# A new order of instructions from the hand-over to the experts on, with two weight subtractions moved from VectorE to GpSimd

## The chip, the core and the metric

The kernel runs on one core of a Trainium2 chip. The metric is the device time of one execution in microseconds. The engines are named as the profile names them: PE is TensorE's matmul side and PEld its weight load, DVE is VectorE, ACT is ScalarE, POOL is GpSimd, SP is SyncE, which issues most DMAs.

## What is computed

Three stages follow each other on 3072 tokens (4 batches of 768) of width 320: a gated linear attention with 8 heads, a dense layer with a softmax gate and a layer norm, and a mixture of 8 experts in which each token goes to one expert alone. The last stage is the one around the change:

```python
logits = xn @ en.T / tau                 # xn, en: rows and expert vectors divided by their norms
expert_idx = np.argmax(logits, axis=1)
gate_w = probs[np.arange(N), expert_idx] # probs: softmax of the logits
for e in range(E):
    mask = expert_idx == e
    h = np.maximum(x[mask] @ w1[e], 0.0)              # 320 -> 1024
    out[mask] = gate_w[mask, None] * (h @ w2[e])      # 1024 -> 320
```

## The kernel before

**Two halves.** In the first half 24 groups of 128 tokens pass through attention, dense layer and routing. Their output rows (320 numbers, the gate, the expert's number) go to a table `ys` in HBM. Every matmul operand is held as a high part in fp32r (rounded by ACT) and a low part (the rest, by a subtraction), and a product is three matmuls. In the second half the eight experts are worked through in the order of their token counts (ranks 0 to 7); the program fixes the number of rows of each rank (496, 432, 448, 424, 360, 352, 328, 264). For each tile of up to 128 rows of a rank, GpSimd gathers the rows from `ys` with an indirect DMA (L1118, tile `xgr`), PE transposes them (L1129, `txr`), ACT and DVE split them (`exr`), PE multiplies with the first weights (m1, L1152 to L1161, tile `hpu`, eight column blocks f = 0 to 7 of some 8 matmuls), ACT takes the positive part as high part (L1184, tile `uu`), DVE makes the low part (L1190), PE multiplies with the second weights (m2, L1208 to L1210, tile `ypu`), ACT scales with the gate (L1215), and GpSimd scatters the rows to the output (L1222).

**From counts to a gather.** For each of 7 blocks of groups (four of 4 groups, one more of 4, then two of 2: blocks 0 to 6) the routing runs through a chain: the best expert of each row (L776 and the rows behind), its place among the expert's rows by a matmul with counts (L810 to L813, tile `pp`), that place read off (L817, L818), a key (L828 to L832, tiles `key` and `vr`), one-hot rows (L837, L839, tiles `ohr` and `ohv`; by GpSimd for blocks 0 to 5, by DVE for block 6), a matmul that inverts them (L845, `ip`), and an addition to the table `inv` (L848). From `inv` DVE takes the row numbers of the gathers (L1037 to L1041). The first three tiles of rank 0 need blocks 0 to 4 only, so they start early; this part of rank 0 is the unit u0. Its fourth tile of 112 rows (unit u1) and all later ranks need block 6, and so the last link of the chain.

**PE during the chain.** While block 6 goes through the chain, PE works on u0. There m1 writes to two PSUM banks in turn, so that block f+2 starts only when ACT and DVE have split block f. PE has 8 blocks of m1 and the first two of three tiles of m2 to do before it takes the transposition of the fourth tile of rank 0.

**Weights.** The five weight tiles of a rank (0 to 2 first weights, 3 and 4 second weights) come over SP (L1098) into a ring of four slots `raw`. ACT makes the high part (L1102), and an engine given in a table subtracts it (L1109; L1106 for tile 2, which has the work on 64 partitions), which frees the slot:

```python
    def w_lo(R, i, eng):
        if i == 2:
            eng.tensor_tensor(out=R.h[2][64:], in0=R.raw[2][64:], in1=R.h[2][64:].bitcast(F32), op=ALU.subtract)
        else:
            R.l[i] = pools[R.pool].tile([P, wsize(i)], F32R, tag=f"l{i}", name=f"l{R.name}_{i}")
            eng.tensor_tensor(out=R.l[i], in0=R.raw[i], in1=R.h[i].bitcast(F32), op=ALU.subtract)
```

**The order.** The kernel is recorded as steps (`plan.add`), each with an engine. A table `AT` gives each step a number, and the steps are written out in the order of these numbers, so that each engine's queue is that order and nothing is reordered at run time. The dependences stay; a step that isn't ready holds all that stands behind it on its engine. Queues touched by the change: PE, DVE, ACT, POOL and SP.

Of the kernel before, what the change touches and what calls it, by code (L numbers as in the profile page):

```python
# [24 lines left out]
E = 8  # L25
# [44 lines left out]
    "ld_c2": "386",  # L70
    "ld_e": "60",
    "set_m": "0",
    "set_z": "28",
    "sets": "1",
    "mk": "63",
    "mku": "520",
# [5 lines left out]
    "bad": "805",  # L82
    "badp": "904",
    "badc": "972",
    "neg": "64",
    "f_in": "546 70 429 10",
    "dec_in": "669 195 597 90",
    "whi": "708 248 668 680 130",
    "wlo": "725 572 704 738 380",
    "wd": "337",  # L90
    "emb1": "171",
    "emb2": "185",
    "embr": "244",
    "emb3": "261",
    "emb4": "279",
    "emb5": "293",
    "f_out": "141 266",
    "dec_out": "318 459",
    "wtr": "494 463 409 450 601 608 618 544",
    "wtc": "510 475 441 464 647 625 637 598",  # L100
    "ep": "576 662",
    "epc": "721",
    "ept": "731",
    "cmb": "1115",
    "eg": "751",
    "eohi": "760",
    "eolo": "827",
    "onefr": "31",
    "ohi": "451 405 413 421 569 545 561 553",
    "olo": "808 786 756 831 765 795 841 817",  # L110
    "cm": "910 915 921 927 933 1092 1099 1104",
    "fill": "62 79 96 114 154 251 289 298 419 477",
    "load_q": "30 115 87 359 332 531 908 1069 1322 1544 1726 1949 2120 2354 2531 2804 3009 3332 3600 3780 4050 4223 4450 4673",
    "load_n": "206 236 399 50 499 577 963 1159 1389 1578 1813 2024 2208 2420 2570 2876 3150 3397 3676 3816 4120 4310 4515 4738",
    "vprep": "355 371 534 385 616 699 1046 1244 1473 1661 1898 2124 2313 2504 2653 2995 3241 3481 3778 3900 4206 4394 4598 4843",
    "tprep": "351 370 533 162 615 698 1070 1275 1472 1667 1897 2121 2293 2503 2654 2960 3258 3485 3781 3925 4205 4393 4614 4822",
    "smat": "131 259 387",
    "pv": "374 436",
    "smm": "486 527",
    "pmul": "168 181 291 305 432 445 882 958 1043 1057 1296 1384 1527 1598 1711 1725 1923 1937 2094 2108 2328 2341 2505 2519 2785 2798 2994 3021 3306 3320 3574 3588 3754 3872 4024 4126 4204 4230 4435 4510 4758 4780 4878 4919 5062 5163 5343 5449",  # L120
    "state": "498 583 909 1100 1323 1738 1950 2144 2355 2535 3036 3333 3601 3804 4051 4462 4686 4891 5077 5356",
    "den": "400 540 902 1123 1316 1541 1776 1978 2161 2382 2532 2840 3113 3361 3629 3774 4044 4218 4449 4702 4933 5106 5384 5552",
    "og": "411 552 938 1135 1363 1553 1788 2000 2184 2394 2544 2852 3125 3373 3651 3790 4081 4285 4490 4714 4945 5128 5396 5564",
    "xdup": "437 578 962 1160 1388 1577 1818 2048 2212 2419 2569 2942 3156 3419 3702 3817 4122 4309 4514 4767 4989 5176 5460 5588",
    "xtr": "470 696 1065 1318 1413 1586 1839 2116 2252 2430 2584 3005 3185 3454 3776 3908 4219 4342 4530 4781 5008 5198 5476 5597",
    "xh": "485 727 1079 1334 1429 1597 1849 2130 2273 2449 2605 3026 3201 3494 3791 3935 4236 4353 4577 4791 5018 5209 5497 5619",
    "xl": "586 775 1098 1352 1447 1611 1863 2173 2287 2462 2627 3040 3219 3508 3812 3948 4249 4366 4591 4806 5051 5267 5511 5654",
    "mm1": "742 806 942 974 1113 1227 1372 1420 1601 1642 1770 1854 1984 2025 2220 2259 2397 2436 2684 2716 2893 2925 3108 3237 3421 3469 3644 3686 3867 3919 4103 4135 4311 4367 4545 4579 4748 4787 4943 4975 5130 5251 5444 5483 5658 5690 5860 5892",
    "negmax": "857 1019 1271 1502 1687 1899 2070 2303 2481 2760 2969 3282 3550 3730 4000 4179 4411 4622 4840 5026 5305 5527 5759 5937",
    "expo": "886 1047 1300 1539 1715 1927 2098 2332 2512 2789 3004 3310 3578 3758 4028 4213 4439 4651 4869 5055 5333 5556 5788 5966",  # L130
    "umul": "914 1074 1328 1573 1742 1954 2125 2358 2589 2815 3051 3337 3605 3823 4056 4260 4466 4677 4895 5081 5360 5584 5814 5992",
    "lnstat": "943 1102 1356 1602 1771 1982 2153 2393 2618 2844 3080 3365 3633 3851 4106 4289 4494 4706 4923 5110 5388 5613 5843 6022",
    "lnvar": "971 1136 1393 1631 1823 2011 2186 2424 2664 2873 3161 3394 3665 3888 4136 4318 4523 4735 4953 5151 5417 5650 5879 6067",
    "lnrs": "1000 1164 1422 1676 1852 2040 2216 2453 2693 2902 3288 3423 3694 3917 4164 4347 4552 4764 4982 5180 5446 5768 5908 6116",
# [8 lines left out]
    "inter": "514",  # L143
    "att": "845 1006 1260 1488 1675 1886 2057 2291 2468 2748 2957 3269 3538 3717 3987 4167 4398 4610 4828 5014 5292 5515",
    "mmp": "5722 5926",
    "rlog": "2020 2927 3685 4602 5478 6027 6222",
    "rnorm": "2068 2939 3722 4621 5490 6046 6234",
    "ridx": "2029 2935 3693 4647 5486 6035 6231",
    "rexp": "2140 2999 3800 4681 5550 6108 6304",
# [1420 lines left out]
```

## Time and profile before

| what | us |
|---|---|
| three runs: median (lowest to highest) | 524.79 (520.2 to 525.45) |
| the profiled execution, its own time | 522.23 |
| its span from the first to the last instruction | 520.4 |
| PE busy, of the span | 494.0 |
| DVE, ACT, POOL busy | 340.0, 275.0, 203.9 |

PE is the engine that is nearly always busy. The time is PE's work and the stretches in which PE waits, so the waits of PE, what ends them, and the granted clock are what is to be read.

### The profile page before, as it was taken

The page shows a single profiled execution, that of the slowest core. Times are in us where ns is not written, and L with a number is a line of the kernel's source. Part 1 is how long each engine was busy: PE and PEld are TensorE (multiplying, and loading weights), DVE is VectorE, ACT ScalarE, POOL GpSimd, SP SyncE. Part 2 cuts the span into 40 slices and gives each one's busy share as a digit, 9 for nine tenths or more (in the row PEclk, how much of TensorE's full clock was granted, in tenths as well). Part 3 has the DMA queues.
Part 4 walks back from the last instruction along what each step waited for, and adds up shares of the span by engine and source line. Part 5 has one row for each costly group of instructions (what it writes and reads, how often), then busy time and mean ns, then how long its engine had stood idle before and what let it go on. Part 6 is the DMA issues. An engine that isn't in the chain of part 4 may idle for free. (4 is left out here: it accounts for less than half of the span.)

```text
span 520.4 us, 14487 instructions
## 1 busy us (share of the span) xinstructions
PE 494.0 (95%) x5925; PEld 452.2 (87%) x5925; DVE 340.0 (65%) x735; ACT 275.0 (53%) x604; POOL 203.9 (39%) x350
## 2 busy tenths in 40 slices
PE   6869999999999999999999899999999999999991
PEld 5747998888899999889898789898999999999991
DVE  5997667777677587677778778677463655485120
ACT  3572555665656556666467565554543644565220
POOL 3221223266246247345315683656172444112021
PEclk9989999999999999999999899999999999999996
DMA  8962233343341253414041412835631861563000
GB/s 300 412 223 81 80 83 120 113 147 111 90 144 46 77 156 121 144 40 143 3 171 44 152 47 96 276 84 193 231 92 44 285 223 64 217 189 121 14 21 31
DMA packets 20139, 68.01 MB, mean 131 GB/s; under 512 B 2658, under 2 KB 6050, under 8 KB 19680
## 3 DMA queue, kind: packets, MB, share of 16 engines
q1 hardware_dynamic: 17120, 58.27, 33.5%
q0 software_dynamic: 2944, 8.73, 5.3%
q8 instruction: 49, 0.80, 0.7%
q14 instruction: 26, 0.21, 0.1%
HBM read 58.31 MB, written 8.72 MB: 129 GB/s over the span
## 5 line engine op out<-in xcount | busy, mean ns | idle before, releaser
L1222 POOL DMA_INDIRECT out_x<-you,sidx x28 | 30.8, 1099 | 95.5 <-ACT you L1215 82.9
L748 PE MATMUL Y<-OH,uh 128*128 128x328 f32 x192 | 63.4, 330 | 0.0
L1190 DVE SCALAR_TENSOR_TENSOR lu<-hpu,uu 128x384 fp32r<-128x384 f32 (+4 forms) x56 | 28.6, 519 | 53.0 <-ACT uu L1184 43.5
L750 PE MATMUL Y<-OH,ul 128*128 128x328 f32 x192 | 60.3, 314 | 0.2 <-DVE ul L740 0.2
L749 PE MATMUL Y<-OL,uh 128*128 128x328 f32 x192 | 60.4, 315 | 0.0
L1208 PE MATMUL ypu<-hr,uu 128*128 128x320 f32 (+4 forms) x192 | 60.1, 313 | 0.0
L1209 PE MATMUL ypu<-lr,uu 128*128 128x320 f32 (+4 forms) x192 | 59.3, 309 | 0.0
L1184 ACT ACTIVATE uu<-hpu 128x384 fp32r<-128x384 f32 (+7 forms) x64 | 30.4, 483 | 52.2 <-PE hpu L1161 40.0
L1109 DVE TENSOR_TENSOR lr<-raw,hr 128x1024 fp32r<-128x1024 f32 (+1 forms) x32 | 43.4, 1355 | 15.1 <-ACT hr L1102 15.1
L1210 PE MATMUL ypu<-hr,lu 128*128 128x320 f32 (+4 forms) x168 | 51.8, 309 | 0.0
L1102 ACT CAST hr<-raw 128x1024 fp32r<-128x1024 f32 (+1 forms) x40 | 45.2, 1134 | 10.5 <-DMA raw<-in_w 9.4
L736 ACT CAST uh<-tpu 128x512 fp32r<-128x512 f32 x48 | 27.7, 586 | 38.7 <-PE tpu L732 38.4
L704 ACT ACTIVATE e<-H,nmx 128x1024 f32<-128x1024 f32 x24 | 26.8, 1117 | 40.2 <-DVE nmx L699 40.2
L1118 POOL DMA_INDIRECT xgr<-ys,gidx x28 | 36.5, 1302 | 27.3 <-issue 8.9
L699 DVE TENSOR_REDUCE nmx<-H 128x1 f32<-128x1024 f32 x24 | 29.4, 1224 | 26.1 <-PE H L695 24.5
L1157 PE MATMUL hpu<-exr,hr 128*128 128x384 f32 (+7 forms) x128 | 43.7, 341 | 0.0
L1158 PE MATMUL hpu<-exr,lr 128*128 128x384 f32 (+7 forms) x128 | 42.5, 332 | 0.0
L1159 PE MATMUL hpu<-exr,hr 128*128 128x384 f32 (+7 forms) x128 | 42.4, 332 | 0.0
L686 PE MATMUL H<-WH,xh 128*128 128x512 f32 x96 | 40.7, 424 | 1.2 <-DVE u L709 1.1
L740 DVE TENSOR_TENSOR ul<-tpu,uh 128x512 fp32r<-128x512 f32 x48 | 32.4, 687 | 12.6 <-ACT uh L736 12.5
L687 PE MATMUL H<-WL,xh 128*128 128x512 f32 x96 | 37.9, 395 | 0.1
L748 PEld LDWEIGHTS Y<-OH,uh 128*128 128x128 f32 x192 | 36.2, 189 | 2.0 <-ACT yr L766 0.2
(230 smaller groups left out, 1351.3 us busy)
## 6 DMA issues: line engine op xcount, KB each, us to landing
qk<-in_qkT SPq DMA_DIRECT2D x24, 512.0 KB, 4.2
raw<-in_w SPq DMA_DIRECT2D x24, 512.0 KB, 4.7
nat<-in_nat SPq DMA_DIRECT2D x24, 484.0 KB, 3.7
raw<-in_w SPq DMA_DIRECT2D x16, 640.0 KB, 5.3
ys<-yr SPq DMA_DIRECT2D x5, 772.0 KB, 5.0
raw<-in_w_out SPq DMA_DIRECT2D x2, 1280.0 KB, 9.3
raw<-in_w_in SPq DMA_DIRECT2D x3, 512.0 KB, 6.4
raw<-in_w_in SPq DMA_DIRECT2D x1, 1024.0 KB, 8.3
```

The lines of the kernel that those rows point to most:

```text
L686: T.matmul(out=o, lhsT=xh[:, kk, :], rhs=WH[:, kk, f], start=(kk == 0), stop=False)
L748: T.matmul(out=yp, lhsT=uh, rhs=OH[:, k, :], start=(k == 0), stop=False)
L749: T.matmul(out=yp, lhsT=uh, rhs=OL[:, k, :], start=False, stop=False)
L750: T.matmul(out=yp, lhsT=ul, rhs=OH[:, k, :], start=False, stop=(k == 7))
L1102: A.copy(out=R.h[i], in_=R.raw[i])
L1109: eng.tensor_tensor(out=R.l[i], in0=R.raw[i], in1=R.h[i].bitcast(F32), op=ALU.subtract)
L1157: T.matmul(out=o, lhsT=R.h[k][:, fs_], rhs=xh[:, k, tk], start=(k == 0), stop=False)
L1158: T.matmul(out=o, lhsT=R.l[k][:, fs_], rhs=xh[:, k, tk], start=False, stop=False)
L1159: T.matmul(out=o, lhsT=R.h[k][:, fs_], rhs=xl[:, k, tk], start=False, stop=False)
L1208: T.matmul(out=yp, lhsT=uh, rhs=hi, start=(f == 0), stop=False)
L1209: T.matmul(out=yp, lhsT=uh, rhs=lo, start=False, stop=False)
L1210: T.matmul(out=yp, lhsT=ul, rhs=hi, start=False, stop=(f == 7))
```

## The change

The numbers of the table `AT` are new from the first steps on, and the engine table of the weight subtractions names GpSimd (`G`) for tiles 1 and 2 of rank 1:

```diff
-    "okr": "2329 2418 2281 2360 3311 ... 6143 6176 6349 6360",
+    "okr": "2246 2279 2359 2311 3360 ... 6159 6191 6309 6335",
-    "cnt2": "6497",
+    "cnt2": "6445",
...
-    lo_eng = [("V", "V", "V", "V", "V")] * E
+    lo_eng = [("V", "G", "G", "V", "V") if r == 1 else ("V",) * 5 for r in range(E)]
```

What this does to the queues is seen at three places.

The first is DVE's queue while PE works on m1 of u0. `rt`, `pp` and `oh` are block 6's places, `key` and `vr` its key, `ohr`/`ohv` its one-hot rows, and `uu_f` the low part of column block f of u0. Before:

```order
L1190 SCALAR_TENSOR_TENSOR uu_1_5071<-hpu_1_5047,uu_1_5071 128x384
L848 TENSOR_TENSOR inv<-inv,ip_5061 128x192
L817 TENSOR_TENSOR rt_4968<-pp_5095,oh_5084 128x2x8
L818 TENSOR_REDUCE rt_4968<-rt_4968 128x2
L1190 SCALAR_TENSOR_TENSOR uu_2_5108<-hpu_2_5073,uu_2_5108 128x384
L828 SCALAR_TENSOR_TENSOR key_5115<-yr_4969,rt_4968 128x2
L829 TENSOR_SCALAR key_5115<-key_5115 128x2
L830 TENSOR_SCALAR key_5115<-key_5115 128x2
L832 CAST vr_5119<-key_5115 128x4
L1190 SCALAR_TENSOR_TENSOR uu_3_5130<-hpu_3_5099,uu_3_5130 128x384
```

The same place of DVE's queue in the changed kernel:

```order
L1190 SCALAR_TENSOR_TENSOR uu_1_5084<-hpu_1_5045,uu_1_5084 128x384
L817 TENSOR_TENSOR rt_4976<-pp_5094,oh_5073 128x2x8
L818 TENSOR_REDUCE rt_4976<-rt_4976 128x2
L828 SCALAR_TENSOR_TENSOR key_5111<-yr_4977,rt_4976 128x2
L829 TENSOR_SCALAR key_5111<-key_5111 128x2
L830 TENSOR_SCALAR key_5111<-key_5111 128x2
L832 CAST vr_5115<-key_5111 128x4
L837 TENSOR_SCALAR ohr_0_5119<-cs,vr_5115 128x128
L839 TENSOR_SCALAR ohv_0_5121<-cs,vr_5115 128x192
L1190 SCALAR_TENSOR_TENSOR uu_2_5123<-hpu_2_5075,uu_2_5123 128x384
L837 TENSOR_SCALAR ohr_1_5128<-cs,vr_5115 128x128
L839 TENSOR_SCALAR ohv_1_5130<-cs,vr_5115 128x192
```

The key and the first one-hot pair now stand ahead of the low part of block 2; before, the low part came first, and the one-hot rows stood behind the low part of block 4. Behind this piece the additions to `inv` and the row numbers also come earlier (ahead of block 5's low part; before, behind block 6's), the subtraction of rank 1's tile 1 is gone from between, and the count, matmul `cnt2` on PE and the second ranking (L1007 to L1016) come ahead of block 7's low part instead of behind it.

The second is POOL's queue from the end of block 6's gate work (L785 to L787) to the first gathers that need block 6 (`xgr_3` of rank 0, then rank 1's). Before:

```order
L785 TENSOR_TENSOR rt_4968<-rt_4968,pw 128x2
L786 TENSOR_TENSOR rt_4968<-rt_4968 128x2x8
L787 TENSOR_TENSOR rt_4968<-rt_4968 128x2x8
L1118 DMA xgr_3_5213<-ys,gidx 112x386
L1118 DMA xgr_0_5229<-ys,gidx 128x386
L1118 DMA xgr_1_5249<-ys,gidx 128x386
L1222 DMA out_x<-you_0_5251,sidx 3072x320
```

The same place of POOL's queue in the changed kernel, with the two moved subtractions:

```order
L787 TENSOR_TENSOR rt_4976<-rt_4976 128x2x8
L1106 TENSOR_TENSOR hr_2_5091<-raw,hr_2_5091 64x1024
L1109 TENSOR_TENSOR lr_1_5141<-raw,hr_1_5098 128x1024
L1118 DMA xgr_3_5201<-ys,gidx 112x386
L1118 DMA xgr_0_5213<-ys,gidx 128x386
L1118 DMA xgr_1_5232<-ys,gidx 128x386
L1118 DMA xgr_2_5248<-ys,gidx 128x386
L1118 DMA xgr_3_5273<-ys,gidx 48x386
```

Both subtractions stand between block 6's gate work and the gathers, and all four gathers of rank 1 now go out ahead of the first scatter.

The third is PE's queue where block 4's places (`pp`) are found, on which the one-hot rows of block 4 on POOL wait. `num` is the end of the last attention step, `Y` the product that closes a group's dense layer, `H` the one that opens it. Before:

```order
L637 MATMUL num_4569<-nat_3898,Pt_4461 32x41 x32
L642 MATMUL num_4569<-Cb_115,qk_3864 32x82 x16
L810 LDWEIGHTS ubf
L810 MATMUL pp_4620<-oh_4556,ubf 128x32
L811 LDWEIGHTS onebf
L811 MATMUL pp_4620<-cum,onebf 128x32
```

The same matmuls in the changed kernel:

```order
L748 MATMUL Y_4620<-OH,uh_1_4523 128x328
L749 MATMUL Y_4620<-OL,uh_1_4523 128x328
L750 MATMUL Y_4620<-OH,ul_1_4537 128x328
L810 LDWEIGHTS ubf
L810 MATMUL pp_4670<-oh_4560,ubf 128x32
L811 LDWEIGHTS onebf
```

They stood directly behind the last attention step and now stand behind the 24 `Y` matmuls of a group. On DVE two of rank 0's weight subtractions (L1109) follow directly around the next `Yc` behind block 4's key; before, three were spread over the time of the one-hot rows.

Further on, the row numbers of ranks 2 to 7 and with them rank 2's gathers come earlier: before, they were computed behind u1's sums, now ahead of the split of the fourth tile of rank 0. On PE rank 1's first two tiles are transposed later than the third and fourth. In the first 60 us a few loads, memsets and transpositions change places.

## Rows read from the trace of the kernel before

**Rows 1.** The profile's page: busy us, share of the span and instructions of each engine.

```profile
PE 494.0 (95%) x5925; PEld 452.2 (87%) x5925; DVE 340.0 (65%) x735; ACT 275.0 (53%) x604; POOL 203.9 (39%) x350
```

**Rows 2.** Timeline of PE (start us, us, instruction, idle before and releaser), 279 to 510 us.

```profile
279.28 0.19 PE L810 MATMUL pp<-oh,ubf 128*128 128x32 bf16 x1
...
292.18 0.47 PE L845 MATMUL ip<-ohv,ohr 128*128 128x192 f32 x2 [1.89 <-POOL ohv L839]
...
331.46 0.29 PE L1129 MATMUL txr<-cs,xgr 112*128 112x112 f32 x1 [1.12 <-DMA xgr<-ys,gidx]
...
353.04 0.55 PE L1129 MATMUL txr<-cs,xgr 128*128 128x128 f32 x3 [0.43 <-DMA xgr<-ys,gidx]
...
355.81 0.37 PE L1129 MATMUL txr<-cs,xgr 64*128 64x64 f32 x3 [0.66 <-DMA xgr<-ys,gidx]
...
509.31 0.30 PE L1209 MATMUL ypu<-lr,uu 128*128 128x320 f32 x1
509.45 0.31 PE L1210 MATMUL ypu<-hr,lu 128*128 128x320 f32 x1
```

**Rows 3.** Busy time by stretch, 292 to 300 us; PEclk is the granted clock.

```profile
292.00:296.00 4.00, 3.82 (x19) 3.77 (x20) 0.78 (x5) 0.38 (x1) 2.24 (x7) 0.69 0.67 244
296.00:300.00 4.00, 4.00 (x19) 3.24 (x17) 3.74 (x10) 3.63 (x8) 0.99 (x3) 0.89 0.00 0
```

**Rows 4.** Timeline of POOL, 283 to 293 us: block 4's one-hot rows.

```profile
283.38 0.63 POOL L837 TENSOR_SCALAR ohr<-cs,vr 128x128 fp32r<-128x128 f32 x1 [0.74 <-DVE rt L803]
...
287.25 1.62 POOL L837 TENSOR_SCALAR ohr<-cs,vr 128x128 fp32r<-128x128 f32 x1
...
291.13 1.00 POOL L839 TENSOR_SCALAR ohv<-cs,vr 128x192 fp32r<-128x192 f32 x1
```

**Rows 5.** Timeline of DVE, 284 to 290 us: one weight subtraction of rank 0.

```profile
286.91 1.48 DVE L1109 TENSOR_TENSOR lr<-raw,hr 128x1280 fp32r<-128x1280 f32 x1
```

**Rows 6.** Timeline of PE, 315 to 318 us: first matmul of u0's m1 block 3, then of block 4.

```profile
315.65 0.42 PE L1157 MATMUL hpu<-exr,hr 128*128 128x384 f32 x1
...
317.12 0.34 PE L1157 MATMUL hpu<-exr,hr 128*128 128x384 f32 x1
```

**Rows 7.** Timeline of DVE, 316 to 325 us.

```profile
316.03 0.17 DVE L818 TENSOR_REDUCE rt<-rt 128x2 f32<-128x16 f32 x1
316.28 0.56 DVE L1190 SCALAR_TENSOR_TENSOR uu<-hpu,uu 128x384 fp32r<-128x384 f32 x1
316.75 0.15 DVE L828 SCALAR_TENSOR_TENSOR key<-yr,rt 128x2 int32<-128x2 f32 x1
...
317.28 0.17 DVE L832 CAST vr<-key 128x4 f32<-128x4 int32 x1
...
319.70 0.28 DVE L837 TENSOR_SCALAR ohr<-cs,vr 128x128 fp32r<-128x128 f32 x1
...
321.16 1.22 DVE L1109 TENSOR_TENSOR lr<-raw,hr 128x1024 fp32r<-128x1024 f32 x1
```

**Rows 8.** Timeline of POOL, 315 to 326 us.

```profile
315.96 0.22 POOL L787 TENSOR_TENSOR rt<-rt 128x16 f32<-128x16 f32 x1
324.25 1.10 POOL L1118 DMA_INDIRECT xgr<-ys,gidx  x1 [8.06 <-DVE sidx L1041]
```

**Rows 9.** Timeline of POOL, 19 to 32 us: values scaled by a gate, both operands in SBUF.

```profile
19.27 3.70 POOL L615 TENSOR_TENSOR nat<-nat,gw 128x328 f32<-128x328 f32 x3 [7.53 <-ACT gw L367]
...
31.38 0.74 POOL L615 TENSOR_TENSOR nat<-nat,gw 128x328 f32<-128x328 f32 x1 [1.97 <-DMA nat<-in_nat]
```

**Rows 10.** Timeline of DVE, 22 to 33 us.

```profile
22.28 1.03 DVE L660 SCALAR_TENSOR_TENSOR og<-nat,den 128x320 f32<-128x320 f32 x1
...
24.95 0.82 DVE L397 TENSOR_SCALAR of<-raw 128x1280 int32<-128x1280 int32 x1
...
29.43 0.49 DVE L660 SCALAR_TENSOR_TENSOR og<-nat,den 128x320 f32<-128x320 f32 x1
...
31.50 1.17 DVE L397 TENSOR_SCALAR wf<-raw 128x1024 int32<-128x1024 int32 x1
```

220 rows, old and new, of the table AT are left out of this document.

## The prediction

> **What bounds the kernel now.** I read the page first: PE is busy for 494.0 of 520.4 us [rows 1], so the program can only gain what PE spends waiting or at half clock, and it loses whatever a new order makes PE wait. So the second view was PE's timeline, read for its idle marks alone. Between 60 and 280 us it has none; nothing is to be won there, and something only to be lost. The marks of the part that the change aims at are four [rows 2]: 1.89 us at 292.18, where PE needs one-hot rows from POOL, and three waits for gathered rows, 1.12 us at 331.46, 0.43 at 353.04 and 0.66 at 355.81. The reader is to see that the last three name a DMA and the first an engine that should have been done long before. The third view was busy time by stretch: behind the wait of 1.89 us the granted clock is 0.69 and 0.89 in two stretches of 4 us [rows 3], so some work ran at 1.2 instead of 2.4 GHz; that lost 0.31 x 4 + 0.11 x 4 = 1.7 us. Behind the wait of 1.12 us no such loss shows. After that I went to DVE and POOL in the two places where PE waits for them.
>
> **Term 1: the gathers.** All three waits for rows go if the rows are asked for earlier. For the first one the gather was issued at 324.25 [rows 8] and released PE at 331.46, some 7.2 us later, and PE had come 1.12 us too early. In the new order the key, the one-hot rows, the additions to `inv` and the row numbers come ahead of low parts that stood before them, and the subtraction of 1.22 us at 321.16 [rows 7] is gone from between. Counted from the key's start this brings the gather some 2 us forward, which is more than 1.12. For rank 2 the row numbers come ahead of the fourth tile's split, and all of rank 1's gathers go out ahead of the first scatter. I take all three waits as gone: -1.12 - 0.43 - 0.66 = -2.2 us. Bounds: -2.2 and 0, if the rows land no earlier relative to PE.
>
> **Term 2: block 4's one-hot rows.** PE's 1.89 us at 292.18 ended with POOL's last one-hot row, 291.13 + 1.00 = 292.13 [rows 4]. POOL began at 283.38 and needs 0.63 + 1.00 = 1.63 us for a pair, 6.5 us for four; it took 8.75. The 2.2 us between are holds: an `ohr` that takes 0.63 alone took 1.62 at 287.25, from the time that DVE ran a weight subtraction, 286.91 to 288.39 [rows 4, 5]. In the new order block 4's places are found not at 279.28 but behind 24 more matmuls of some 0.15 us each (one starts 0.14 us behind the other at the end [rows 2]), at 282.9. DVE needs some 1.5 us from there to the key's end (in block 6 from 316.03 to 317.45 [rows 7]), so POOL begins at about 284.4, 1.0 us later. Two subtractions now follow directly on the key, so I leave the holds at 2.2 us. What PE has to do ahead of that point is the same set of steps, so PE goes on 1.0 us later: +1.0. Bounds: -3.6 if the wait and its 1.7 us of slow clock go (fewer subtractions beside POOL), +2.5 if every pair is held.
>
> **Term 3: m1 of u0.** PE has no spare time here: block f+2 needs the low part of block f. Block 3 began at 315.65 and block 4 at 317.12 [rows 6], just when block 2's low part had ended at 316.84 [rows 7], without a wait. In the new order this low part has the key (316.75 to 317.45, 0.70 us) and the first one-hot pair (0.28 and its partner, 0.49 us together as from 319.70 on [rows 7]) ahead of it. These can begin at 316.2, when the places are read off. The low part then ends at 316.2 + 0.70 + 0.49 + 0.56 = 318.0, block 4 can start at 318.1, and PE waits 1.0 us. Later, the count matmul stands ahead of block 7 and needs DVE's count, which now stands behind block 5's low part; I estimate 0.4 us for this (bounds 0 and 1.0). +1.4 together.
>
> **Term 4: the two subtractions on POOL.** No row shows them there. The bounds are DVE's 1.22 us for the same shape [rows 7] and, by POOL's slowest elementwise row per element (1.00 us for 192 [rows 4]), 5.3 us. Nearest is POOL's product of two SBUF tensors, 0.74 us for 328 columns [rows 9]: 0.74 x 1024 / 328 = 2.3 us each; I take that. On POOL they fill time in which it was idle: its gate work ended at 316.18 and the next gather came at 324.25 [rows 8], so 4.6 us fit and end about when the gather's row numbers are there. DVE loses 2.4 us of work, which counts in term 1. What they cost is on DVE. Rows show that POOL holds DVE too: the product at 22.28 took 1.03 us beside three POOL products from 19.27 to 22.97, the same one at 29.43 took 0.49; and a step with one input, 1024 wide, took 1.17 us at 31.50 beside POOL's product from 31.38, where 1280 columns took 0.82 [rows 9, 10]. Now the first subtraction comes to POOL at 316.2 (or a little earlier), and the key's first instruction has two SBUF inputs and comes to DVE at 316.2. If POOL is first, the key waits until nearly its end: 1.7 to 2.1 us, and with it the one-hot pair and block 2's low part, on which PE waits. I take 1.9 us, all of it on PE's path, which is without spare time. Bounds: 0, and 4.6 for both subtractions. PE then waits 2.9 us at one place, longer than the 1.89 us behind which the clock fell, so I add the same 1.7 us (bounds 0 and 3).
>
> The Trainium skill, page "SBUF — State Buffer", section "Who interferes with whom", says that a DVE instruction with two SBUF inputs contends with a GpSimd instruction that reads SBUF, and that the loser waits for the whole of the other instruction. The rows at 22.28 and 29.43 agree with it. By that rule term 4 is the 1.9 us above; without it, it would be 0.
>
> **The rest.** The first 60 us have the same steps with a few changed places: 0, bounds -1.5 and +1.5 (the waits there are loads and one chain of small steps, and nothing in the new order lengthens it). Behind the last matmul at 509.45 nothing changes. The middle stays full: 0.
>
> **Sum.** -2.2 + 1.0 + 1.4 + 1.9 + 1.7 = +3.8 us. On the profiled execution's 522.23 us (span 520.4) this is 526.0. The median of the three runs, 524.79, is 2.6 us above that execution, and the lowest is 2.0 below; I keep 526.0 and let the range take the difference. A measurement of this kernel can tell about 1%, 5.2 us, from no change.
>
> **Rivals.**
> No hold: the key slips in ahead of POOL's subtraction. For it: the two come to their engines within a few tenths. Against it: POOL's gate work could only end earlier, since the one-hot rows before it are freed by a key that isn't later. Then term 4 and its clock go: 526.0 - 1.9 - 1.7 = 522.4. Chance 0.27.
>
> Two holds, the slower side: behind the first subtraction POOL starts the second at once, and the rest of the key (a conversion with its input and output in SBUF) or the one-hot row is held by it. For it: the one-input step at 31.50 was held. Against it: the key's remaining steps have two or four columns, and a step already waiting may go first. The price is one more subtraction, 2.3 us, on PE's path: 528.3, and with a longer slow stretch up to 530. That is 6.1 us above 522.23; it decides as soon as the key's conversion ends behind the second subtraction's end. Chance 0.19.
> The Trainium skill, same page and section, has copies, casts and single-input scalar steps among those that can take both ports; no run here shows it for so small a step. By that rule this rival holds.
>
> All waits go: the two subtractions next to block 4's key end before POOL's one-hot rows need the port, and neither hold happens. Then -2.2 - 1.9 - 1.7 + 1.0 or less: 517 or a little lower. For it: a wait that is not there costs no clock. Against it: the places are found 3.6 us later. Chance 0.10.
>
> The gathers land no earlier: the weights of rank 1 are asked for at about the same time and share the DMA engines. Then term 1 is 0 beside the rest: 528.2. Against it: PE itself comes later by terms 2 to 4. Chance 0.04.
>
> **How the numbers follow.** The forecast has 0.40, its own range is 523.5 to 529. Faster by over 1% needs below 517 on this execution's base, the third rival and half a chance of runs that fall low: 0.11. Slower by over 1% needs above 527.5: the two holds, the late gathers and a fifth of the forecast: 0.29. Within 1%: 0.60. The range of 520 to 531.5 leaves out the all-waits-go case and the far end of two holds.
>
> **What would show it.** Right: no wait for gathered rows at u1's and rank 2's transpositions; PE idle at the first matmul of u0's block 4 by 2 to 3 us with DVE's low part as releaser; DVE's L828 of block 6 at some 2 us instead of 0.15 beside POOL's L1106; the granted clock below 1 behind it; POOL's L1106 and L1109 of about 2.3 us; block 4's one-hot rows ending at about 293 and PE's wait for them. Wrong: L828 short and block 4 waiting 1 us or less (no hold); a wait at the gathered rows that stays; new idle marks between 60 and 280 us, which I have at nothing; or a start that differs by more than 1.5 us.

## The result and the profile after

| | before | after |
|---|---|---|
| median of 6 runs each (lowest to highest), us | 525.12 (520.2 to 525.79) | 530.27 (528.12 to 533.02) |
| ratio, 95% interval | 1 | 1.011 (1.0074 to 1.0147) |
| the profiled execution, its span, us | 522.23, 520.4 | 528.12, 526.4 |

The change made the kernel slower by 1.1%. To find the place, the span is cut at four rows of PE's timeline that every kernel of this text has: the last attention step (L642, 32 matmuls), the first m1 matmul of u0 (`hpu` with 384 columns), the first of u1 (`hpu` with 112 columns) and the last matmul.

| stretch, us | before | after |
|---|---|---|
| start to the last attention step | 278.58 | 278.18 |
| from there to u0 | 32.33 | 34.58 |
| u0 to u1 | 23.06 | 28.51 |
| u1 to the last matmul | 175.48 | 174.00 |

So 2.25 us went ahead of u0, 5.45 in u0, and 1.48 came back behind it. The page of the profile after says little of this: PE is busy for 3.3 us more, at a mean granted clock of 0.974 instead of 0.985, and the other engines are nearly as before [rows 1].

```profile
PE 497.3 (94%) x5925; PEld 454.7 (86%) x5925; DVE 342.1 (65%) x733; ACT 276.6 (53%) x604; POOL 203.0 (39%) x352
```

PE's timeline after the change, the rows that answer to [rows 2] (in brackets the idle time before a row and what released it):

```profile
289.05 0.42 PE L750 MATMUL Y<-OH,ul 128*128 128x328 f32 x1 [0.78 <-DVE ul L740]
291.33 0.35 PE L845 MATMUL ip<-ohv,ohr 128*128 128x192 f32 x1 [0.52 <-POOL ohv L839]
292.91 0.58 PE L845 MATMUL ip<-ohv,ohr 128*128 128x192 f32 x3 [1.22 <-POOL ohv L839]
...
310.56 0.55 PE L1129 MATMUL txr<-cs,xgr 128*128 128x128 f32 x3 [0.94 <-DVE exr L1141]
...
323.85 0.69 PE L1157 MATMUL hpu<-exr,hr 128*128 128x384 f32 x1 [4.86 <-DVE uu L1190]
...
339.10 0.45 PE L1129 MATMUL txr<-cs,xgr 112*128 112x112 f32 x3
...
515.27 0.30 PE L1210 MATMUL ypu<-hr,lu 128*128 128x320 f32 x1
```

The three waits for gathered rows are gone: the row at 339.10 has no bracket, nor has any later one for a gather. In their place stands one wait of 4.86 us at u0's block 4, for VectorE's low part. Behind it the granted clock, the third column from the end, is at the lower of its two levels:

```profile
320.00:324.00 4.00, 0.15 (x1) 0.15 (x1) 3.86 (x8) 0.00 (x0) 2.61 (x2) 0.66 0.00 0
324.00:328.00 4.00, 4.00 (x14) 4.00 (x15) 2.22 (x9) 0.49 (x1) 0.00 (x0) 0.50 0.49 132
```

VectorE was kept from the low part by its key. Its timeline, to be read against [rows 7], where the key's steps take 0.15 to 0.17 us each:

```profile
317.89 0.16 DVE L828 SCALAR_TENSOR_TENSOR key<-yr,rt 128x2 int32<-128x2 f32 x1
318.08 2.22 DVE L829 TENSOR_SCALAR key<-key 128x2 int32<-128x2 int32 x1
...
320.47 2.24 DVE L832 CAST vr<-key 128x4 f32<-128x4 int32 x1
...
323.24 0.55 DVE L1190 SCALAR_TENSOR_TENSOR uu<-hpu,uu 128x384 fp32r<-128x384 f32 x1
```

And POOL's, which answers to [rows 8]:

```profile
317.88 2.39 POOL L1106 TENSOR_TENSOR hr<-raw,hr 64x1024 fp32r<-64x1024 f32 x1
320.35 2.34 POOL L1109 TENSOR_TENSOR lr<-raw,hr 128x1024 fp32r<-128x1024 f32 x1
...
329.82 1.10 POOL L1118 DMA_INDIRECT xgr<-ys,gidx  x1 [7.13 <-DVE sidx L1041]
```

L829 works on two numbers per partition and ends (320.30) when L1106 ends (320.27); L832 ends (322.71) when L1109 ends (322.69). The short L830 slipped in between the two. Each subtraction held one step of the key for nearly its whole length. In this text a hold is just that: a step has its operands and yet ends only when the other engine's instruction does.

Ahead of u0, POOL's one-hot rows of block 4 after the change, first pair and last row (compare [rows 4]):

```profile
284.19 1.68 POOL L837 TENSOR_SCALAR ohr<-cs,vr 128x128 fp32r<-128x128 f32 x1 [1.41 <-DVE vr L832]
285.87 2.26 POOL L839 TENSOR_SCALAR ohv<-cs,vr 128x192 fp32r<-128x192 f32 x1
...
291.85 1.01 POOL L839 TENSOR_SCALAR ohv<-cs,vr 128x192 fp32r<-128x192 f32 x1
```

and VectorE beside them (compare [rows 5]):

```profile
284.15 1.22 DVE L1109 TENSOR_TENSOR lr<-raw,hr 128x1024 fp32r<-128x1024 f32 x1
...
285.76 1.48 DVE L1109 TENSOR_TENSOR lr<-raw,hr 128x1280 fp32r<-128x1280 f32 x1
```

Here VectorE holds POOL: the first pair takes 3.94 us, a free one 0.63 + 1.00 [rows 4]. The rows end at 292.86.

### The profile page after: what moved, and what is told of

Read it like the earlier page. It is cut to its first block, busy times and chain, and to the rows that moved or that the text cites. A ratio compares the mean times of both kernels' runs of the same rounds, so it can differ in the third digit from the quotient of the medians.

```text
span 526.4 us, 14485 instructions
## 1 busy us (share of the span) xinstructions
PE 497.3 (94%) x5925; PEld 454.7 (86%) x5925; DVE 342.1 (65%) x733; ACT 276.6 (53%) x604; POOL 203.0 (39%) x352
## 5 line engine op out<-in xcount | busy, mean ns | idle before, releaser
L1109 DVE TENSOR_TENSOR lr<-raw,hr 128x1280 fp32r<-128x1280 f32 (+1 forms) x31 | 41.9, 1359 | 30.8 <-ACT hr L1102 27.4
L1222 POOL DMA_INDIRECT out_x<-you,sidx x28 | 29.4, 1049 | 81.8 <-ACT you L1215 63.9
L1190 DVE SCALAR_TENSOR_TENSOR lu<-hpu,uu 128x384 fp32r<-128x384 f32 (+4 forms) x56 | 29.0, 520 | 41.2 <-ACT uu L1184 40.9
L1157 PE MATMUL hpu<-exr,hr 128*128 128x384 f32 (+7 forms) x128 | 44.8, 350 | 4.9 <-DVE uu L1190 4.9
L1159 PE MATMUL hpu<-exr,hr 128*128 128x384 f32 (+7 forms) x128 | 43.1, 336 | 0.0
L719 ACT ACTIVATE e<-u,nmx 128x1024 f32<-128x1024 f32 x24 | 29.9, 1245 | 15.9 <-POOL nmx L715 15.9
```

What stands on the lines that cost most here:

```text
L1157: T.matmul(out=o, lhsT=R.h[k][:, fs_], rhs=xh[:, k, tk], start=(k == 0), stop=False)
L1159: T.matmul(out=o, lhsT=R.h[k][:, fs_], rhs=xl[:, k, tk], start=False, stop=False)
```

## The experiments

Theory: the loss in u0 is the two holds of the key, what the order costs there without them, and the clock behind the wait; ahead of u0 it is the order. Main rival: the new order costs all of it, whoever subtracts. In the table, "start" ends at the last attention step, and "wait" is PE's at u0's block 4. The ratio is to the kernel before, with its 95% interval.

| kernel | median, us | ratio | start | to u0 | u0 to u1 | u1 to end | wait |
|---|---|---|---|---|---|---|---|
| before | | 1 | 278.58 | 32.33 | 23.06 | 175.48 | 0 |
| after | 530.27 | 1.011 | 278.18 | 34.58 | 28.51 | 174.00 | 4.86 |
| e1, both on VectorE | 527.43 | 1.0065 (1.0016 to 1.0113) | 277.58 | 34.55 | 24.44 | 177.41 | 1.99 |
| e2, both there, late | 530.22 | 1.0074 (1.0042 to 1.0105) | 281.27 | 35.20 | 29.42 | 174.20 | 0.76 |
| e3, one on GpSimd | 530.72 | 1.0113 (1.0041 to 1.0184) | 279.86 | 35.28 | 27.76 | 174.24 | 2.98 |
| e4, before with GpSimd | 531.62 | 1.0127 (1.0054 to 1.02) | 281.08 | 30.70 | 23.45 | 183.90 | 1.50 |
| e5, splice | 530.43 | 1.0121 (1.0078 to 1.0165) | 281.56 | 32.25 | 28.84 | 175.12 | 4.92 |
| e6, one pair moved | 530.47, one run | | 279.91 | 34.48 | 28.91 | 174.15 | 4.90 |
| e7, behind the key | 532.75, one run | | 281.96 | 35.14 | 26.97 | 175.71 | 2.91 |
| e8, gathers first | 524.0 | 0.9979 (0.9953 to 1.0005) | 282.13 | 32.22 | 23.49 | 174.09 | 0 |
| e9, and weights behind | 521.93 | 0.9942 (0.9914 to 0.9971) | 280.12 | 32.23 | 21.92 | 175.31 | 0 |
| e10, and two holds of POOL less | 521.51 | 0.9901 (0.9866 to 0.9936) | 282.07 | 30.56 | 21.96 | 178.41 | 0 |
| e11, and all gathers first | 522.26 | 0.993 (0.9906 to 0.9954) | 282.28 | 30.56 | 21.86 | 174.38 | 0 |
| e12, these two less, alone | 524.18 | 0.9975 (0.9946 to 1.0004) | 281.83 | 30.55 | 22.57 | 175.93 | 0 |

The first column of stretches warns of whole times: kernels that have the same order up to there reach the last attention step anywhere from 278.6 to 282.3 us (before, e4, e5, e8 to e12), and those with the new order from 277.6 to 282.0. A single profile tells a total badly, and a stretch only together with its granted clock: up to u0 e4 has the order of before, and took 30.70 us instead of 32.33.

**e1: both subtractions back on VectorE.**

```diff
-    lo_eng = [("V", "G", "G", "V", "V") if r == 1 else ("V",) * 5 for r in range(E)]
+    lo_eng = [("V", "V", "V", "V", "V")] * E
```

> The changed order kept, the two subtractions of rank 1 back on VectorE at their places in it (tile 2's behind the key, ahead of the first one-hot pair; tile 1's behind the second one-hot pair). Theory (what costs is that VectorE's key is held twice by GpSimd): VectorE now does the 2 x 1.2 us itself at nearly the places where it was held 2 x 2.1 us, so L829 and L832 take some 0.15 us each, block 4 of u0 waits about 2.5 us instead of 4.86, and the time falls by 2 to 3 us, to about 528. Rival (the order costs, whoever subtracts): the wait at block 4 falls too, but less than 1 us arrives at the end, 529.5 to 531.

Measured as the theory has it: the wait is 1.99 us, the clock behind it stays at 1.00, u0 takes 4.07 us less, and the median is 2.8 us less, though the intervals of the two ratios overlap. In the profiled pair only 0.7 us of it is left at the last matmul (236.40 us from the last attention step, 237.09 after the change), since PE now comes sooner than the gathered rows of rank 1. PE's timeline of e1:

```profile
320.33 0.44 PE L1157 MATMUL hpu<-exr,hr 128*128 128x384 f32 x1 [1.99 <-DVE uu L1190]
...
338.09 0.55 PE L1129 MATMUL txr<-cs,xgr 128*128 128x128 f32 x3 [0.35 <-DMA xgr<-ys,gidx]
...
339.86 0.38 PE L1129 MATMUL txr<-cs,xgr 48*128 48x48 f32 x3 [1.22 <-DMA xgr<-ys,gidx]
```

Behind the last of these the granted clock of the next 4 us is 0.58, and u1 to the end takes 3.4 us more than after the change.

**e2: both on VectorE and late.** e1 and, in the table (the loads that need the freed slots go along):

```diff
-    "wo": "... 6553 6345 6297 6666 6521 ...",
+    "wo": "... 6553 6423 6511 6666 6521 ...",
```

> The changed order, both subtractions of rank 1 on VectorE and behind the low parts of u0's blocks 5 and 7, so that nothing of them lies between the key and block 2's low part. Theory (holds): block 4's wait falls from 4.86 to about 1 us, the clock behind it stays near full, no wait for gathered rows comes back or one below 0.5 us, so 530.3 - 3.9 - 1.9 = about 524.5, level with the kernel before. Rival (the order of the matmuls and one-hot rows ahead of u0 and behind it costs the time): the wait goes but the time stays above 527.5.

The wait at block 4 came as said, 0.76 us; the time did not. The edit made two waits of its own. The first subtraction now stood ahead of the count, and the weights that need its slot came late to ACT, in whose queue u0's output stands behind them. PE's timeline of e2:

```profile
324.35 0.45 PE L1157 MATMUL hpu<-exr,hr 128*128 128x384 f32 x1 [0.76 <-DVE uu L1190]
...
330.26 0.18 PE L1003 MATMUL cnt<-cum,onebf 128*128 128x8 bf16 x1 [1.18 <-DVE cum L823]
...
342.44 0.63 PE L1208 MATMUL ypu<-hr,uu 128*128 128x320 f32 x1 [3.16 <-ACT you L1215]
```

So 0.76 us is what the changed order costs at block 4 without a hold. The time is above 527.5, as the rival has it, but 4.34 us of it are the two waits that the edit made, so the total decides nothing.

**e3: one subtraction on GpSimd.** Tile 2's stays, tile 1's goes behind block 5's low part on VectorE (three loads, not shown, go along):

```diff
-    lo_eng = [("V", "G", "G", "V", "V") if r == 1 else ("V",) * 5 for r in range(E)]
+    lo_eng = [("V", "V", "G", "V", "V") if r == 1 else ("V",) * 5 for r in range(E)]
-    "wo": "... 6553 6345 6297 6666 6521 ...",
+    "wo": "... 6553 6423 6297 6666 6521 ...",
```

> The changed order, tile 2's subtraction alone on GpSimd (64 partitions), tile 1's on VectorE behind block 5's low part. Theory (each subtraction holds the key's step that stands at VectorE's head, for its whole length): one hold, L829 again 2.2 us beside L1106, L832 about 0.2 us, block 4 waits 2.5 to 3 us, the time lies about 2.5 to 3 us below the changed kernel, 527 to 528. Rival (half as many partitions or one instruction alone does not hold): L829 below 0.3 us and block 4 waits 1 us, as with both on VectorE.

One hold and a wait of 2.98 us, as expected; the held step was another. L1106 ran from 321.08 to 323.45, and L828, the step with two SBUF inputs, came 0.02 us behind its start. VectorE's timeline of e3:

```profile
321.10 2.38 DVE L828 SCALAR_TENSOR_TENSOR key<-yr,rt 128x2 int32<-128x2 f32 x1
323.51 0.17 DVE L829 TENSOR_SCALAR key<-key 128x2 int32<-128x2 int32 x1
```

After the change L828 came 0.01 us behind it and was not held, L829 was. Which step pays changes between two nearly equal starts; that one pays does not. The starts in the trace do not tell which: in e7 a step that began 0.07 us ahead of L1106 was held. The granted clock stayed at 1.00 behind this wait. The time missed its 527 to 528 because tile 1's new place brought e2's wait at the count again (1.18 us) and 0.83 us for ACT at 340.93.

**e4: the order of before, the two on GpSimd.** Only the engine table is that of the changed kernel.

> The order of before, only the engine of the two subtractions changed to GpSimd at their places of before. There GpSimd reaches the first of them behind block 5's and 6's gate work and VectorE has other small steps at its head. Theory (a hold needs a small step that comes to VectorE while the subtraction runs; its price is what PE then waits): one or two small VectorE steps of 0.15 us take 1 to 2.3 us, PE waits 0 to 2 us at block 4 or 5, and the freed 2.4 us of VectorE bring the gather of rank 0's fourth tile nearer; 524 to 527. Rival (moving them to GpSimd is harmless in itself and the new order is what costs): no long small step, 522 to 524.5.

The hold is there in the old order too, beside POOL's L1109 (318.13 for 2.37 us). VectorE's timeline of e4:

```profile
318.15 2.38 DVE L832 CAST vr<-key 128x4 f32<-128x4 int32 x1
...
333.70 0.51 DVE L1141 TENSOR_TENSOR exr<-txr,exr 128x336 fp32r<-128x336 f32 x1 [1.19 <-ACT exr L1136]
```

The second row shows what is not held: L1141 has one operand in PSUM, ran from 333.70 inside L1106 on POOL (331.90 for 2.87 us) and took its usual 0.51. The time is above both expectations for a reason that I had not named. In POOL's queue L1106 stood between rank 1's first and second gather, began 2.90 us late (the profile names a gather's landing as what it waited for; why it needs that was not tried), the second gather went out only at 335.04, and PE waited 5.35 us for rank 1's rows at 341.75. Moving work to an engine with idle time moves it into that engine's queue.

This profile shows one thing more. Up to u0 its order is that of before, POOL's rows of block 4 take as long (8.74 us), and PE waits the same 1.89 us for them, but the clock behind the wait did not fall. PE's timeline of e4 and the two stretches from 292 us, to be read against [rows 2] and [rows 3]:

```profile
294.67 0.47 PE L845 MATMUL ip<-ohv,ohr 128*128 128x192 f32 x2 [1.89 <-POOL ohv L839]
...
292.00:296.00 4.00, 2.11 (x15) 1.94 (x15) 2.38 (x4) 2.46 (x3) 3.65 (x7) 1.00 0.50 133
296.00:300.00 4.00, 4.00 (x26) 3.56 (x25) 2.97 (x6) 2.57 (x6) 1.25 (x4) 1.00 0.35 140
```

The stretch to u0 is 30.70 us, 1.6 less than before. In the other profiles with this order and this wait (before, e5, e8, e9) the clock fell and the stretch is 32.2 to 32.3.

**e5: the order of before ahead of u0, the new one from there on.**

Steps with a number below 6165 in the kernel before keep it; all later ones have the changed kernel's number plus 20000. Two rows of the table, and the engine table:

```diff
-    "key": "2264 3159 3959 4793 5617 6126 6287",
+    "key": "2264 3159 3959 4793 5617 6126 26295",
-    "cnt2": "6497",
+    "cnt2": "26445",
...
-    lo_eng = [("V", "V", "V", "V", "V")] * E
+    lo_eng = [("V", "G", "G", "V", "V") if r == 1 else ("V",) * 5 for r in range(E)]
```

> All steps that stand ahead of u0's first m1 block in the order of before, all later ones in the order of the changed kernel, the two subtractions on GpSimd. Theory (the loss is two separate parts, 2.2 us ahead of u0 and 5.4 us in u0): the stretch from the last hidden attention step (L637) to u0's first m1 is again that of before, 33.0 us instead of 35.2; u0 to u1 stays 28 to 28.5 us with block 4's wait of 4.5 to 4.9; the time is 530.3 - 2.2 = about 528. Rival (the stretch ahead of u0 depends on what follows, or gives its 2.2 us back at u0): no gain, 530.

The stretch to u0 is 32.25 us again, and u0 keeps its 28.84 with a wait of 4.92: the two losses are separate. The median did not fall with it, 530.43 where the theory had 528, so that the loss ahead of u0 is seen in the stretch and not in the time. The start of this profile was 3.4 us longer than that of the profile after; over all profiles the starts with the old order lie 1.4 us above those with the new one (mean of eight 281.2, of six 279.8). With a spread of 4 us in each that is a hint, not a finding, that the new first 60 us gain what the stretch to u0 loses.

**e6: rank 0's tile 2 behind the split.**

```diff
-    "wh": "5674 5625 6068 ...",
-    "wo": "5887 5691 6092 ...",
+    "wh": "5674 5625 6089 ...",
+    "wo": "5887 5691 6118 ...",
```

> The changed kernel with one pair moved: the conversion (ACT) and the subtraction (VectorE, L1106) of rank 0's weight tile 2 behind the split of the first gathered tile instead of ahead of it. Theory (the 0.94 us wait of the third transposition at 310.56 comes from that pair standing ahead of the split): that wait goes or falls below 0.2 us and the stretch from L637 to u0's first m1 falls from 35.2 to about 34.3 us. Rival (u0's first m1 block needs that tile anyway): the wait moves to u0's first block and the stretch stays at 35 us.

The wait of 0.94 us is gone and came back at the products behind. PE's timeline of e6:

```profile
311.29 0.42 PE L748 MATMUL Y<-OH,uh 128*128 128x328 f32 x1 [0.29 <-ACT uh L736]
312.78 0.42 PE L750 MATMUL Y<-OH,ul 128*128 128x328 f32 x1 [0.93 <-DVE ul L740]
```

The stretch is 34.48 us beside 34.58: the wait moved. The two executions differ in one more thing. After the change the clock fell behind the one-hot rows (0.75 and 0.83 from 292 to 300 us), in e6 it stayed at 1.00 up to u0; PE came sooner and waited longer for VectorE (1.01 us at 302.72, where it had been 0.30), and the stretch stayed. So the fallen clock costs little in this part of the new order, where PE waits for VectorE anyway, and at full clock the new order is here 3.8 us longer than the old one (34.48 in e6, 30.70 in e4), not 2.25. Which step of the new order makes it so was not found.

**e7: GpSimd begins only when the key is done.** A copy of one number of the key goes ahead of the subtractions:

```diff
-        vr = s["vr"] = small.tile([P, 2, n], F32, tag="vr", name="vr" + name)
+        vr = s["vr"] = pools["kv"] = small.tile([P, 2, n], F32, tag="vr", name="vr" + name)
...
-                add(("wo", r, i), eng, lambda R=R, i=i, eng=eng: w_lo(R, i, V if eng == "V" else G), ...
+                add(("wo", r, i), eng, lambda R=R, i=i, eng=eng: (G.tensor_copy(out=small.tile([P, 1], F32, tag="kvc", name="kvc")[:1], in_=pools["kv"][:1, 0, 0:1]) if eng == "G" and i == 2 else None, w_lo(R, i, V if eng == "V" else G)), ...
```

> The changed kernel with one tiny GpSimd copy ahead of its two subtractions that reads block 6's key, so that GpSimd begins them only when the key is done. Theory (any VectorE step with operands in SBUF alone that could use the second port is held, one step for each subtraction): L828 to L832 take 0.15 us each, and the one-hot rows behind (L837 of 0.28 us, L839 of 0.37 us) take over the two holds of 2.2 us; block 4 waits 4 to 5 us as before this edit. Rival (only the tiny key steps are held): the one-hot rows keep 0.28 and 0.37 us and block 4 waits about 1 us.

The key took its 0.15 to 0.17 us a step, and the next steps of the same kind paid. VectorE's timeline of e7, beside L1106 (324.23 to 326.57) and L1109 (326.65 to 329.02):

```profile
324.16 2.53 DVE L839 TENSOR_SCALAR ohv<-cs,vr 128x192 fp32r<-128x192 f32 x1
326.61 0.55 DVE L1190 SCALAR_TENSOR_TENSOR uu<-hpu,uu 128x384 fp32r<-128x384 f32 x1
327.08 2.03 DVE L837 TENSOR_SCALAR ohr<-cs,vr 128x128 fp32r<-128x128 f32 x1
```

Two holds, as the theory says, but the low part of block 2 (its input `hpu` is in PSUM) ran between them untouched, so only the first one lay ahead of it: PE waited 2.91 us, not 4 to 5. The time did not gain by it; there was one run, and it has a wait of 1.95 us for gathered rows at 347.52.

**e8: the old order, gathers first.** From here on the aim is a kernel that has the change's gain without its costs. It is the kernel before, with rank 1's tile 1 subtracted behind the row numbers (and its loads and conversions later), and ranks 2 and 3's row numbers earlier:

```diff
-    "wl": "... 6411 5324 5819 6418 6425 ...",
+    "wl": "... 6460 5324 5819 6461 6462 ...",
-    "wh": "... 6489 6272 6235 6524 6558 ...",
+    "wh": "... 6511 6272 6235 6524 6605 ...",
-    "wo": "... 6563 6382 6477 ...",
+    "wo": "... 6563 6459 6477 ...",
-    "col_2": "6816",
+    "col_2": "6540",
```

> The order of before with few steps moved, all subtractions on VectorE: rank 1's subtraction of tile 1 goes behind block 6's row numbers and the count instead of ahead of them (with the three loads that follow it in the ring of raw weights, and ACT's conversions of these behind its first output and behind the splits of the gathered rows), and the row numbers of ranks 2 and 3 come directly behind the second ranking, where VectorE is idle. Theory (the aim of the change without its costs): the gather of rank 0's fourth tile is issued 1.2 us earlier, the waits of 1.12, 0.43 and 0.66 us go, and the time is 525.1 - 2.2 = about 523, with the stretch from u0 to u1 22 us instead of 23.1. Rival (the weights that now come 2.6 us later hold ACT, as in the run with both subtractions late): new waits of 1 to 3 us for ACT between 330 and 345 us, 525 to 527.

No wait for gathered rows is left, and the rival came as well. PE's timeline of e8:

```profile
337.64 0.37 PE L1152 MATMUL hpu<-exr,hr 128*128 128x224 f32 x1 [1.44 <-DVE exr L1141]
```

ACT kept the split back: a conversion of a late weight tile stood ahead of it (335.44 for 1.26 us, after 1.05 of waiting for its DMA).

The waits did not go for the reason given. Counted from u0's first m1 the gather of rank 0's fourth tile was issued 13.14 us later, before it was 13.34: 0.2 us earlier, not 1.2. But it landed 3.2 us after its issue instead of 7.1. The next weight loads on SP begin 2.0 us behind it (329.49 against 327.49); before, they began 1.75 us ahead of it (322.50 against 324.25), and in e12, with the loads as far ahead (323.97 against 325.71), it took 6.5. That the loads make the difference is argued; no run moved them alone.

**e9: those conversions behind the splits.**

```diff
-    "wh": "... 6511 6272 6235 6524 6605 ...",
+    "wh": "... 6511 6272 6235 6605 6798 ...",
-    "wo": "... 6563 6459 6477 6890 6628 ...",
+    "wo": "... 6563 6459 6477 6890 6812 ...",
```

> The run with the gathers first, with ACT's conversions of rank 1's tiles 3 and 4 moved from ahead of, and between, the splits of the gathered rows to behind them, and VectorE's subtraction of tile 4 behind u1's sums. Theory (the 1.44 us wait at u1's first m1 block comes from a conversion that waits for its late weights ahead of the split of rank 0's fourth tile): that wait goes, u0 to u1 takes about 22 us instead of 23.5 (23.1 before), the time is 524.0 - 1.4 = about 522.6. Rival (PE waits for the same conversions later, at the second product of rank 1): a wait for ACT or VectorE of 1 us or more between 345 and 365 us and 524 again.

The wait is gone, u0 takes 21.92 us, and the kernel is faster than the one before beyond its interval.

**e10: two of the three subtractions away from POOL's one-hot rows of block 4.** Rank 0's tiles 0 and 4 go behind them, and one load with them:

```diff
-    "wl": "5294 5288 5812 ...",
+    "wl": "5294 5288 5817 ...",
-    "wo": "5784 5665 5965 5856 5720 ...",
+    "wo": "5815 5665 5965 5856 5816 ...",
```

> The run before this one and, ahead of u0, two of rank 0's three weight subtractions (tiles 4 and 0, L1109) moved from beside GpSimd's one-hot rows of block 4 to behind them, where VectorE is idle. Theory (each subtraction holds a one-hot row by 0.7 to 1.0 us, and PE waits for the last row): GpSimd's eight rows take 7.1 us instead of 8.8, PE's wait of 1.89 us falls to 0.2 to 0.5 us and the clock behind it rises, so the stretch from L637 to u0 falls from 33.0 to 30.5 to 31.3 us and the time by 1.7 to 2.5 us, to about 520.5. Rival (the holds come from other VectorE steps, or the later weights make u0 wait): the stretch stays at 32.5 us or more.

POOL's eight rows took 7.0 us (286.87 to 293.89), PE waited 0.17 us for them, and the stretch to u0 is 30.56, 1.67 less than in e9. That is not the wait. Most of it came back a little later, in waits for VectorE. PE's timeline of e10:

```profile
300.82 0.17 PE L1003 MATMUL cnte<-cum,onebf 128*128 128x8 bf16 x1 [0.49 <-DVE ul L740]
306.43 1.06 PE L732 MATMUL tpu<-cs,u 128*128 128x128 f32 x8 [1.22 <-DVE u L709]
```

The first of these was not there in e9, and the second was 0.28. What is gained is the clock, which is 1.00 from 292 to 300 us here and 0.75 and 0.82 in e9. With the wait of 1.89 and a full clock e4 took 30.70, so the wait by itself is worth some 0.15 us. In this profile rank 1's 48-row tile was then late: a wait of 0.76 us at 339.55. The two stretches behind it show what that cost (granted clock third from the end):

```profile
340.00:344.00 4.00, 3.91 (x23) 3.72 (x24) 1.40 (x6) 1.64 (x7) 2.98 (x3) 0.69 0.30 87
344.00:348.00 4.00, 4.00 (x18) 4.00 (x18) 2.15 (x7) 2.98 (x7) 1.98 (x2) 0.50 0.47 133
```

0.31 x 4 + 0.50 x 4 = 3.2 us behind a wait of 0.76. The gather of that tile was issued as long ahead of u1 as in e9 (1.86 us), where PE did not wait for it. This execution took 525.57 us, the other five 519.09 to 521.97.

**e11: all of rank 1's gathers ahead of the first scatter,** as the change has them.

```diff
-    "xg": "... 6476 6501 6560 6585 ...",
+    "xg": "... 6476 6501 6502 6503 ...",
```

> The run before this one, with the last two gathers of rank 1 (tiles 2 and 3) issued ahead of the first scatter, as the changed kernel has them. Theory (the 0.76 us wait for rank 1's 48-row tile at 339.55 is a gather that came 4 us after the first, and the half clock behind it, 0.69 and 0.50 in the next two stretches of 4 us, is paid for that wait): the wait goes, the granted clock from 340 to 348 stays at 0.95 or more, u1 to rank 1 takes 9.8 us as in the kernel before instead of 14.0, and the profiled time is near 521; the median falls below 521.5. Rival (more gathers at once land later together): the fourth tile of rank 0 is waited for instead, 521.5 to 523.

The wait is gone, the clock from 340 to 348 is 1.00, and the twelve runs lie between 521.4 and 523.59. As e9 had no such wait either, without this edit, one profile does not show that the edit removed it. The median is not below e10's; e9, e10 and e11 can't be told apart, and all three beat both kernels.

**e12: e10's edit alone, on the kernel before.**

> The kernel before with one edit: the two subtractions of rank 0 (tiles 4 and 0) behind GpSimd's one-hot rows of block 4. Theory (what the new order lost and the old one loses at this place is the hold, and it is worth its clock too): the stretch from L637 to u0 is 31.2 us instead of 33.0 as in the run with both edits, the waits of 1.12, 0.43 and 0.66 us for gathered rows stay, and the time is 525.1 - 1.8 = about 523.3. Rival (without the earlier gathers PE comes to the transpositions earlier and waits there for what it won): the wait of 1.12 us grows, 524.5 to 525.

The stretch to u0 is 30.55 us, 1.8 less than before and 0.15 less than in e4, and its clock is 1.00. So what the two moved subtractions gain is nearly all the clock: behind the wait of 1.89 us it fell in four profiles of five, without that wait in none of three (e10 to e12). Waits for gathered rows of 0.56, 0.30, 0.37 and 0.77 us remain. The time is 1.6 us lower, with an interval that just reaches 1, so that the whole time does not show the gain for certain.

## Why the prediction was right, and where not

The time, 530.27, lies in the range, but not with the likeliest case: 526.0 was for one hold, and it was the rival with two (528.3 to 530, chance 0.19) that came; the profiled execution, the one that the sum is for, took 528.12. So the range held by a case that I thought unlikely. I gave most to a change within 1%; it is 1.1% slower. The parts that I named for slower add up to 0.31 (0.19, 0.04 and a fifth of 0.40), not 0.29.

- **Term 1, the gathers (-2.2).** The number was right, and by luck. All three waits went: 1.12 us in u0, and 1.09 of the 1.48 us behind u1 (the rest has no wait to go with it). But "counted from the key's start this brings the gather some 2 us forward" failed. From the key's first step (L828) to the last step of the row numbers (L1041) it was 7.31 us before, 5.48 without a hold (e2, 322.51 to 327.99), and 10.95 after the change, because the holds of term 4, 4.1 us, lie in this very chain and VectorE then waits 1.71 us for PE's `ip` (0.29 in e2). The first gather went out 5.57 us later than before (329.82 against [rows 8]), and its rows were in time because PE came 7.64 us later. e1 shows it: with PE sooner, 1.57 us of waits for gathers return.
- **Term 2, block 4's one-hot rows (+1.0).** Right in its steps: POOL began at 284.19 (I had 284.4), the rows ended at 292.86 (293), the holds of the first pair are 3.94 - 1.63 = 2.3 us (2.2), and PE's last `ip` matmuls came 1.1 us later, counted from the last attention step. What failed is "what PE has to do ahead of that point is the same": behind that point the new order loses another 1.1 us, in waits of 0.30, 0.20 and 0.94 us for VectorE where before had 0.27 and 0.16, and the prediction has no term for it. e5 shows that both go with the old order. That the clock fell behind the wait is not sure either (e4): the lower bound of -3.6 us took a wait and its clock together, and of these the two moved subtractions gave back 1.7 to 1.8 (e10, e12), nearly all of it clock.
- **Term 3, m1 of u0 (+1.4).** The 1.0 us at block 4 is 0.76 without a hold (e2). The 0.4 for the count was nothing: the matmul `cnt2` stands at 330.52 without idle time.
- **Term 4, the subtractions on POOL (+1.9 and +1.7).** The duration was right, 2.39 and 2.34 us where I took 2.3. The step that failed is "the key's remaining steps have two or four columns, and a step already waiting may go first", by which I put two holds at 0.19. Two or four columns are no protection: 2.22 and 2.24 us for steps of 0.17. That L828 would be the one to wait was wrong here and right in e3. The Trainium skill ("SBUF — State Buffer", section "Who interferes with whom") counts casts and single-input scalar steps among those that can take both ports; after, e4 and e7 agree with it (2.24, 2.38, 2.03 us), and I should have given that rule more weight than the two rows that I had. By the same section a step with at most one SBUF input, outside those two-port modes, does not contend: L1141 in e4 and L1190 in e7, which have one input in SBUF and one in PSUM, agree (0.51 and 0.55 us).
- **The clock.** I added 1.7 us for a wait of 2.9. Behind waits of 2.98 (e3), 2.91 (e7) and 1.99 us (e1) at that very place the granted clock was 1.00; behind 4.86 it was 0.50 for one stretch of 4 us, 2.0 us, and behind 4.92 (e5) and 4.90 (e6) it cost 2.3 and 2.5 us, counted from the end of the wait. The size was near the mark, the wait that I tied it to was not: even behind the 1.89 us that I took it from, e4 lost none.
- **The rest (0, within 1.5).** Not contradicted; the starts scatter more than that.

The sum with the measured sizes, for the profiled pair: -1.12 - 1.48 (gathers, and 0.39 without a cause) + 2.25 (ahead of u0) + 0.76 (block 4) + 4.1 (holds: 2.22 + 2.24, less 2 x 0.17) + 2.0 (clock) - 0.4 (start) = 6.1 us, where the last matmul came 5.82 us later.

## What to carry to other kernels

Before work is moved to an idle GpSimd, list the VectorE steps that will run beside it with their operands in SBUF alone: each may wait for one whole GpSimd instruction, however small it is, and the length of the instruction, not of the step, is the price. Put such work beside VectorE steps that read PSUM (two such steps ran untouched here), or where nobody waits for VectorE. The reverse holds, too: with two VectorE subtractions moved away, GpSimd's eight one-hot rows took 7.0 us instead of 8.75. What a shorter wait is worth is seen only where PE's next wait is and what the clock does: there 1.7 us of wait were worth 0.15, and the clock that stayed up 1.6. A wait for a transfer that is gone because the engine comes later is not won: in e1 such waits came back when PE came sooner.

## What the runs showed of the hardware that I had not expected

- A step of 0.17 us on two numbers per partition can be held 2.2 us. Which step it is can't be told from the starts: 0.01 us behind POOL's instruction one was not held (after), 0.02 us behind it one was (e3), and so was one that began 0.07 us ahead of it (e7).
- GpSimd's subtraction takes as long on 64 partitions (2.39 us) as on 128 (2.34).
- The length of one wait does not tell the clock behind it: 0.76 us (e10) was followed by 3.2 us of loss, 1.89 us before the change by 1.7 [rows 3], the same wait at the same place in e4 by none, 2.91 us (e7) by none.
- One and the same gather of 112 rows landed 7.1 us after its issue before the change and 3.2 us in e8.
- Executions of one and the same order up to there differ by up to 3.7 us in when PE comes to the last attention step (278.58 to 282.28). The whole times of the kernel before lie within 5.6 us in the six runs of the first table, and between 520.0 and 530.6 us over all that were taken beside the experiments.
